# Attention followed by a four-expert layer: all four experts' second layer as seven block products, with side work moved between VectorE and GpSimd

## Chip, cores and metric

The kernel runs on one core of a Trainium2 chip. The metric is the device time of one execution in microseconds (us); smaller is better. Every figure below comes from the page of one profiled execution of the kernel before, from its trace, or from the runs' times.

## What is computed

The reference, cut to what matters. First, attention with pooled keys and values (8 batches, 8 heads, 576 queries, width 64, keys and values averaged in groups of 8, so 72 of them):

```python
k_p = k.reshape(B, H, Sp, pool, D).mean(axis=3)
v_p = v.reshape(B, H, Sp, pool, D).mean(axis=3)
scores = scale * np.matmul(q, k_p.transpose(0, 1, 3, 2))
attn = softmax(scores)
x = (attn @ v_p) rearranged to (4608, 512)
```

Then four experts, each a two-layer network of width 512, 1024, 512, weighted by probabilities:

```python
p = domain_probs / (domain_probs.sum(-1, keepdims=True) + 1e-09)
for e in range(4):
    h = np.maximum(x @ w1[e], 0.0)
    out += p[:, e:e + 1] * (h @ w2[e])
```

## The kernel before

**Chunks and steps.** The 4608 tokens are nine chunks `c` of 512: chunk `b` for `b` below 8 holds the first 512 queries of batch `b`; chunk 8 holds the 64 left over from each of the eight batches. A step `s` is a pair `(c, e)`, with `s = 4c + e`. In step `s` TensorE computes the first layer ("up") of `(c, e)` and, interleaved with it, the second layer ("down") of the step before it. While chunk `c` goes through its four steps, the attention of batch `c + 1` is worked in between.

**Block products.** A product of two matrices cut into 2 by 2 blocks can be formed from seven block products in place of eight (the method of Strassen and Winograd), if sums and differences of blocks, here called forms, are ready. The up layer is done so from step 2 on, except for step 4: `product` (L652) issues 4 matmuls of 256 columns for one block and one of two halves `j`, so 2 x 7 x 4 = 56 for a step. It needs forms of the weights (`combine_w1`, L600 to L603) and of x (`forms_of`, L616: four differences of 128x512). The down layer comes in two ways. The plain way (`down`, L850) issues 32 matmuls of 512 columns, and `merge` adds each of the four results into `acc` (VectorE, L867; on ScalarE for expert 0, L864). The split way (`up_down`, with `half`, L777) issues 56 matmuls of 256 columns, again in two halves `j`. It needs forms of w2 (`combine_w2`, L640 to L643, in the tile `w2_t`, with one block of w2 overwritten) and of the hidden layer (`sums_of`, L717 to L720: s1, the difference that overwrites a21, s2 and S4, each 128x1024). The function `splits` says which steps' down layer is split: experts 0, 1 and 2 from chunk 2 on, and experts 1 and 2 of chunk 1, which makes 23 steps.

**The end of a split step.** The last first-layer result of a step comes through `relu_sum` (L700), and the sums follow at once on VectorE: s1, a21, s2, S4. In the next step TensorE runs product 1, half 1, products 5 and 6, and then half 7, which reads a21 as overwritten; half 6 follows with s2, half 5 with s1, and last of the j = 0 half, half 3 with S4.

**Order.** Every engine's order is written out by hand. `up_down` and `between` pass 16 numbered points a step; `attention(c)` lists pieces of work with `add(n, ...)`, and a piece stands at point 2n + 1 of its chunk, so that eight values of n make a step and 32 a chunk. Every second point is also a slot, which takes one piece off the queue `forms_due`. The pieces of the attention of batch `b` are:
- `load_half` (L96): keys and values arrive by DMA issued on GpSimd, in two halves, the second of which is added to the first by the DMA. It can only go when the first has landed.
- `fold_parts` (L211, L216, L219): the rest of the pooling, on VectorE, for keys (into `kp`) and for values (into `vps`).
- `keys` (L233), `queries` (L251), `turn` (L412), `rem_turn`: transposes by DMA from SP, which also issues the stores of the output (L875, L879).
- `loads_wait` (L240): a one-element copy on GpSimd that waits for the transposed keys, and so holds back the loads queued behind it.
- `scores` (L268 on TensorE, L272 on ScalarE), `context` (L391), `divide` (L372, L373), and, in every odd chunk, the same for the left-over queries (`rem_...`).

**Preparation.** The weights arrive in the first 60 us or so. Their forms are made in steps 1 to 8; those of w2 for expert 2 are made on GpSimd in step 5, all others on VectorE.

Of the kernel before, what the change touches and what calls it, by code (L numbers as in the profile page):

```python
# [18 lines left out]
def kernel(  # L19
# [16 lines left out]
    POOL = 8  # L36
# [12 lines left out]
    SPLIT = (0, 1, 2)  # L49
# [25 lines left out]
    w2_t = wpool.tile([P, len(SPLIT), 3, FCH // 2, TH], BF16, name="w2_t")  # L75
# [9 lines left out]
    def load_kv(b, src, nm):  # L85
        wide = (w2_t[0:SP].rearrange("p a b f d -> p (a b f d)")[:, 0:H * POOL * D] if nm == "vraw"
# [70 lines left out]

    NBLK = NCH * NR
# [48 lines left out]
    def fold_parts(nm, b, hs, last):  # L207

        def first():
            raw = raws[(nm, b)]  # L210
            nc.vector.tensor_add(out=raw[:, hs, 0:4, :], in0=raw[:, hs, 0:4, :],  # L211
                                 in1=raw[:, hs, 4:8, :])

        def rest():
            raw = raws[(nm, b)]
            nc.vector.tensor_add(out=raw[:, hs, 0:2, :], in0=raw[:, hs, 0:2, :],  # L216
                                 in1=raw[:, hs, 2:4, :])
            for out in last(hs):
                nc.vector.tensor_add(out=out, in0=raw[:, hs, 0, :], in1=raw[:, hs, 1, :])  # L219
# [3 lines left out]
    def key_parts(b):  # L223
        return [part for hs in halves for part in fold_parts(
            "kraw", b, hs, lambda hs: [kp[0:SP, hs, dup, :] for dup in range(2)])]

    def value_parts(b):
        return [part for hs in halves for part in fold_parts(
            "vraw", b, hs, lambda hs: [vps[b % 3][:, hs, 0:D]])]
# [209 lines left out]
    def rem_scores(i):  # L439
        qTr = state.pop(("qTr", i))  # L440
        two = two_banks()
        for bb in range(2):
# [9 lines left out]
        expTr = apool.tile([SP, 2, 2, NPAIR, REM], BF16, name="expTr", bufs=1)  # L452
        nc.scalar.activation(
            out=expTr[:].rearrange("j a b h t -> j (a b h t)"),
# [77 lines left out]
    def attention(c):  # L532
# [8 lines left out]
        if c % 2:  # L541
            i = c // 2
            add(18, lambda: rem_queries(i))
            add(23, lambda: rem_scores(i))
            add(26, lambda: rem_context(i))
            add(27, lambda: rem_turn(i))
        if b == B:
            for part in forms_of(B):
                add(31, part)
            return plan  # L550
        more, far = b + 1 < B, b + 2 < B
        if c == 1:
# [4 lines left out]
            for half in range(2):  # L557
                add(2 + half, lambda half=half: load_half(b + 1, k, "kraw", half))
# [5 lines left out]
        else:  # L564
            for pair in range(NPAIR):
                add(5 + pair, lambda pair=pair: scores(b, pair))
            add(0, key_parts(b)[1], lambda: keys(b))
            for n, part in enumerate(value_parts(b)):
                add(3 + n, part)
            if more:  # L570
                add(0, lambda: loads_wait(b))
                for half in range(2):
                    add(2 + 2 * half, lambda half=half: load_half(b + 1, k, "kraw", half))
# [4 lines left out]
        if more:  # L578
# [446 lines left out]
```

## Time and profile before

| | |
|---|---|
| median of 3 runs | 514.88 us (514.63 to 516.45) |
| profiled execution | 514.31 us; its span from first to last instruction is 512.6 us |
| granted TensorE clock | 0.999 of full speed |
| TensorE matmul busy | 498.9 us, 97% of the span |
| VectorE busy | 370.5 us, 72% |
| ScalarE busy | 274.1 us, 53% |
| GpSimd busy | 72.4 us, 14% |
| DMA | 41.62 MB, mean 81 GB/s |

"Busy" is the time in which an engine executes an instruction. The profile names instructions by engine (PE is TensorE, PEld its loading of weights, DVE VectorE, ACT ScalarE, POOL GpSimd, SP SyncE), by line of the kernel and by tiles, output before input. The chain of waits follows the work that ended last back from the end: at each step to what released an instruction, or to the instruction ahead of it on its engine. The timeline lists instructions in order of time, with start and duration, and in brackets how long the engine had been idle before and who released it.

### The profile page before, as it was taken

The numbers are of one execution on the slowest core, as the hardware profiler recorded it, in microseconds if no ns is written. First come the engines' busy times: TensorE is split into PE (matmuls) and PEld (weight loads), VectorE is DVE, ScalarE is ACT, GpSimd is POOL, SyncE is SP. The second block draws the span as 40 slices with busy tenths as digits, with TensorE's granted clock in tenths as the row PEclk, the third lists the DMA queues.
The fourth block names the chain that finished last, engine by engine and source line by source line (L and its number), as shares of the span: only waits on it lengthen the run. The fifth ranks groups of instructions, "written<-read, shape, count | busy, mean of one in ns | idle before, by whom it ended". The sixth has DMA issues, their size and how long they took to land.

```text
span 512.6 us, 10563 instructions
## 1 busy us (share of the span) xinstructions
PE 498.9 (97%) x4339; PEld 379.0 (74%) x4339; DVE 370.5 (72%) x693; ACT 274.1 (53%) x495; POOL 72.4 (14%) x85
## 2 busy tenths in 40 slices
PE   8899989999999999999999999999999999999996
PEld 4746544578768876888688868886888788868883
DVE  2335788878888877877787868787778567766774
ACT  3654434655466547654566556564765456535650
POOL 8362102740112001100220021000000000000000
PEclk9999999999999999999999999999999999999999
DMA  9999999775179217940597049501210110011003
GB/s 135 205 206 205 202 147 181 125 80 64 41 110 143 27 26 110 137 58 10 107 128 86 1 100 126 58 12 55 62 22 1 42 54 1 12 42 42 0 2 84
DMA packets 82977, 41.62 MB, mean 81 GB/s; under 512 B 46560, under 2 KB 78304, under 8 KB 82928
## 3 DMA queue, kind: packets, MB, share of 16 engines
q0 software_dynamic: 41584, 22.65, 34.8%
q1 hardware_dynamic: 41344, 18.29, 17.6%
q8 instruction: 34, 0.56, 0.4%
q14 instruction: 15, 0.12, 0.1%
HBM read 45.16 MB, written 9.44 MB: 107 GB/s over the span
## 4 chain that ended last, share of the span: by engine, by line
PE 77%; DMA 9%; DVE 8%; POOL 2%; issue 1%; ACT 1%; DVEq 0%; POOLq 0%; ACTq 0%
PE g_ps L652 34%; PE u_ps L777 26%; PE o_ps L850 12%; DMA w_bf<-in_moe_w_dram 4%; DMA q_sb<-in_q_dram 4%; DVE acc L783 2%; PE two L268 2%; DVE H_sb L700 2%; PE h_ps L670 1%; PE two L391 1%; POOL w_bf L148 1%; DVE x_tok L373 1%; DVE h_s L717 1%; DMA xT<-x_tok 1%; DVE xf L616 1%
## 5 line engine op out<-in xcount | busy, mean ns | idle before, releaser
L652 PEld LDWEIGHTS <-w_bf 128*128 128x128 bf16 x1848 | 176.8, 98 | 39.4 <-issue 6.5
L652 PE MATMUL g_ps<-xf,w_bf 128*128 128x256 bf16 x1056 | 148.4, 272 | 1.7 <-ACT g_ps L789 0.7
L696 ACT COPY r<-g_ps 128x512 f32<-128x512 f32 x152 | 89.1, 586 | 77.1 <-PE g_ps L652 66.5
L700 DVE CUSTOM_DVE_ANT_0 H_sb<-g_ps,r 128x512 bf16<-128x512 f32 x152 | 104.3, 687 | 32.4 <-ACT r L696 29.6
L783 DVE SCALAR_TENSOR_TENSOR acc<-u_ps,p_all,acc 128x256 f32<-128x256 f32 (+1 forms) x156 | 91.3, 587 | 41.9 <-ACT u_ps L805 40.9
L850 PE MATMUL o_ps<-w_bf,H_sb 128*128 128x512 bf16 x416 | 104.0, 379 | 0.0
L652 PE MATMUL g_ps<-xT,w_bf 128*128 128x256 bf16 x696 | 101.8, 273 | 0.0
L703 ACT ACTIVATE H_sb<-g_ps 128x512 bf16<-128x512 f32 x112 | 66.8, 597 | 25.0 <-PE g_ps L652 25.0
L777 PEld LDWEIGHTS <-H_sb 128*128 128x128 bf16 x736 | 70.0, 98 | 11.7 <-DVE H_sb L718 2.7
L777 PE MATMUL u_ps<-w_bf,H_sb 128*128 128x256 bf16 x552 | 75.5, 273 | 0.2
L850 PEld LDWEIGHTS <-H_sb 128*128 128x128 bf16 x416 | 40.5, 98 | 31.5 <-issue 0.2
L777 PEld LDWEIGHTS <-h_s 128*128 128x128 bf16 x552 | 54.0, 98 | 6.3
L777 PE MATMUL u_ps<-w_t,h_s 128*128 128x256 bf16 x368 | 55.2, 273 | 0.0
L789 ACT COPY g_ps<-g_ps 128x512 f32<-128x512 f32 x46 | 26.3, 571 | 48.2 <-PE g_ps L652 48.1
L867 DVE SCALAR_TENSOR_TENSOR acc<-o_ps,p_all,acc 128x512 f32<-128x512 f32 x44 | 32.8, 745 | 8.9 <-PE o_ps L850 8.8
L272 ACT ACTIVATE expT<-two 72x1024 bf16<-72x1024 f32 x28 | 28.6, 1021 | 12.5 <-PE two L268 12.5
L805 ACT COPY u_ps<-u_ps 128x256 f32<-128x256 f32 x46 | 16.4, 357 | 25.5 <-PE u_ps L777 25.2
L777 PE MATMUL u_ps<-w_t,H_sb 128*128 128x256 bf16 x184 | 27.7, 273 | 0.0
L777 PE MATMUL u_ps<-w_bf,h_s 128*128 128x256 bf16 x184 | 27.6, 273 | 0.0
L373 DVE TENSOR_TENSOR x_tok<-two,inv 128x512 bf16<-128x512 f32 x32 | 22.1, 691 | 1.1
L807 DVE TENSOR_SCALAR acc<-u_ps,p_all 128x512 f32<-128x512 f32 x14 | 10.5, 750 | 14.1 <-ACT u_ps L805 14.1
L717 DVE TENSOR_TENSOR h_s<-H_sb 128x1024 bf16<-128x1024 bf16 x23 | 15.7, 684 | 5.3 <-ACT H_sb L703 5.3
(112 smaller groups left out, 386.4 us busy)
## 6 DMA issues: line engine op xcount, KB each, us to landing
out_dram<-acc SPq DMA_DIRECT2D x32, 256.0 KB, 2.3
w_bf<-in_moe_w_dram POOLq DMA_DIRECT2D x16, 256.0 KB, 9.8
w_bf<-in_moe_w_dram POOLq DMA_DIRECT2D x4, 1024.0 KB, 16.8
q_sb<-in_q_dram POOLq DMA_DIRECT2D x7, 512.0 KB, 9.3
raw_kv<-in_k_dram POOLq DMA_DIRECT2D x10, 288.0 KB, 6.7
raw_kv<-in_v_dram POOLq DMA_DIRECT2D x10, 288.0 KB, 9.0
raw_kv<-in_k_dram POOLq DMA_DIRECT2D x2, 576.0 KB, 15.8
w_t<-in_v_dram POOLq DMA_DIRECT2D x2, 576.0 KB, 14.3
```

The lines of the kernel that those rows point to most:

```text
L272: nc.scalar.activation(out=state[("expT", b)][:, 2 * pair:2 * pair + 2].rearrange("j h r s p -> j s (h r) p"), in_=two[0:SP].rearrange("j ...
L373: nc.vector.tensor_tensor(out=x_tok[:], in0=c_ps[:, :, :, 0:D], in1=inv[:].unsqueeze(3).to_broadcast([P, 2, NPAIR, D]), op=ALU.mult,)
L652: nc.tensor.matmul(bank[:, t, :], lhsT=w1_bf[:, e, block, kc, lo:lo + P], rhs=x[:, kc, :], start=(first and t == 0 and kc == 0), stop=(t = ...
L696: nc.scalar.copy(out=r[:], in_=ps[:])
L700: nc.vector._custom_dve(TENSOR_ADD_SAT, out=out, in0=ps[:], in1=r[:], s0=BIG, s1=0.0)
L703: nc.scalar.activation(out=out, in_=ps[:], func=ACT.Relu)
L717: lambda: add(out=s1, in0=a21, in1=a22),
L777: nc.tensor.matmul(out, lhsT=lhs[0][:, lhs[1] + f, lhs[2]], rhs=rhs[0][:, rhs[1] + f, rhs[2]], start=(start and f == 0), stop=(f == FCH // ...
L783: nc.vector.scalar_tensor_tensor(out=acc, in0=ps, scalar=prob, in1=acc, op0=ALU.mult, op1=ALU.add,)
L789: nc.scalar.copy(out=s[:], in_=g[:])
L850: nc.tensor.matmul(sums[r][:], lhsT=hidden[(c, e)][:, fc, r * P:(r + 1) * P], rhs=w2_bf[:, e, fc, :], start=(fc == 0), stop=(fc == FCH - 1),)
L867: nc.vector.scalar_tensor_tensor(out=dst, in0=o_ps[:], scalar=prob, in1=dst, op0=ALU.mult, op1=ALU.add,)
```

## The change

**Which steps are split.** `splits` becomes true from (1, 2) up to (8, 2): all four experts of chunks 2 to 7, experts 2 and 3 of chunk 1, experts 0 to 2 of chunk 8. That is 29 steps. Expert 1 of chunk 1 becomes plain; expert 3 of chunks 1 to 7 becomes split. `w2_t` grows to four experts, and the values that borrow it on arrival lie in the part of experts 2 and 3. The last step, expert 3 of chunk 8, stays plain and needs w2 as it was, so the overwritten block is loaded again in step 33. The stores of the output, which `merge` issued, are issued from `up_down` when the expert is the last.

**What changes engine.** S4 goes to GpSimd. From chunk 2 on the forms of x are made on GpSimd, and the last of them is written over a block of x that is no longer needed, in place of a fourth tile. The folds of keys are on GpSimd from batch 3 on. The forms of w2 are all on VectorE, over steps 1 to 8.

**What moves.** In `attention`, `loads_wait` stays for batch 2 only. Scores move to n = 2, 4, 6, 8, loads of keys to 4 and 8, key folds of the next batch to 16 (they were at 31 and at 0 of the next chunk), loads of values to 21 and 27, `keys` to 24, loads of queries to 28, the forms of x to 25 (they were at 22, 25, 28 and 29). The left-over queries of the last chunk move from n = 18, 23, 26, 27 to 2, 10, 13, 14, and their exponentials share a buffer with the others.

The diff, cut to its core:

```diff
-    w2_t = wpool.tile([P, len(SPLIT), 3, FCH // 2, TH], BF16, name="w2_t")
+    w2_t = wpool.tile([P, E, 3, FCH // 2, TH], BF16, name="w2_t")
...
+    def reload_w2(e):
+        rows = moe_w2[e].rearrange("(fc p) d -> p fc d", p=P)
+        nc.gpsimd.dma_start(out=w2_bf[:, e, 4:8, TH:DM], in_=rows[:, 4:8, TH:DM])
...
     def key_parts(b):
+        engine = nc.vector if b == 2 else nc.gpsimd
         return [part for hs in halves for part in fold_parts(
-            "kraw", b, hs, lambda hs: [kp[0:SP, hs, dup, :] for dup in range(2)])]
+            "kraw", b, hs, lambda hs: [kp[0:SP, hs, dup, :] for dup in range(2)], engine)]
...
         if c % 2:
             i = c // 2
-            add(18, lambda: rem_queries(i))
-            add(23, lambda: rem_scores(i))
-            add(26, lambda: rem_context(i))
-            add(27, lambda: rem_turn(i))
+            q_at = 15 if b < B else 2
+            for n, piece in zip((0, 8, 11, 12), (rem_queries, rem_scores, rem_context, rem_turn)):
+                add(q_at + n, lambda piece=piece: piece(i))
+        parts = forms_of(b, nc.gpsimd)
+        add(25, *parts)
...
             for pair in range(NPAIR):
-                add(5 + pair, lambda pair=pair: scores(b, pair))
-            add(0, key_parts(b)[1], lambda: keys(b))
+                add(2 + 2 * pair, lambda pair=pair: scores(b, pair))
             for n, part in enumerate(value_parts(b)):
-                add(3 + n, part)
-            if more:
-                add(0, lambda: loads_wait(b))
-                for half in range(2):
-                    add(2 + 2 * half, lambda half=half: load_half(b + 1, k, "kraw", half))
+                add(4 + n, part)
...
         if more:
+            add(4, lambda: load_half(b + 1, k, "kraw", 0))
             add(11, lambda: queries(b + 1))
-            add(31, key_parts(b + 1)[0])
-            for half in range(2):
-                add(17 + 2 * half, lambda half=half: load_half(b + 1, v, "vraw", half))
+            add(8, lambda: load_half(b + 1, k, "kraw", 1))
+            add(16, *key_parts(b + 1))
+            add(21, lambda: load_half(b + 1, v, "vraw", 0))
+            add(27, lambda: load_half(b + 1, v, "vraw", 1))
+            add(24, lambda: keys(b + 1))
         if far:
-            add(19, lambda: (load_q(b + 2), load_q_rem(b + 2)))
-        for n, part in enumerate(forms_of(b)):
-            add((22, 25, 28, 29)[n], part)
+            add(28, lambda: (load_q(b + 2), load_q_rem(b + 2)))
...
         def last():
-            new(at(1, 0), t[1])
+            engine.tensor_sub(out=at(0, 1), in0=at(1, 1), in1=at(0, 1))
...
     def splits(c, e):
-        return e in SPLIT and (c > 1 or c == 1 and e > 0)
+        return (1, 2) <= (c, e) < (B, E - 1)
...
-            lambda: sub(out=s4, in0=a12, in1=s2),
+            lambda: nc.gpsimd.tensor_sub(out=s4, in0=a12, in1=s2),
...
             elif s == 4:
-                w, x = combine_w1(0), combine_x(1)
-                forms_due.extend(w[:2] + combine_w1(1) + x[:1] + [lambda: (x[1](), w[2]())])
+                v2, x = combine_w2(1), forms_of(1)
+                forms_due.extend(v2[:2] + combine_w1(1))
+                forms_due.extend([lambda: (x[0](), x[1]()), lambda: x[2]()])
             elif s == 5:
-                forms_due.extend(w[3:] + nothing[:2] + combine_w2(1))
-                placed.setdefault(at + 5, []).extend(combine_w2(2, nc.gpsimd))
+                x[3]()
+                forms_due.extend(u[3:] + nothing[:2] + combine_w2(2))
+            elif s == 6:
+                v3 = combine_w2(3)
+                forms_due.extend(nothing[:1] + v3[:1] + nothing[:2] + v3[1:])
+            elif s == 7:
+                forms_due.extend(nothing[:1] + v2[2:3] + nothing[:3] + v2[3:])
             elif s == 8:
-                forms_due.extend(nothing[:1] + combine_w2(0))
+                forms_due.extend(nothing[:1] + w[3:])
+            elif s == E * B + 1:
+                reload_w2(E - 1)
```

Steps 1 and 2 make the forms of chunk 0's x and the first forms of expert 0's weights in the same manner.

## The prediction

> **What bounds the kernel now.** I read the busy table first, then the chain of waits, then busy time by stage, then timelines of the stages that differ. The busy table and the chain's shares by engine, from the page:
>
> ```profile
> PE 498.9 (97%) x4339; PEld 379.0 (74%) x4339; DVE 370.5 (72%) x693; ACT 274.1 (53%) x495; POOL 72.4 (14%) x85
> ...
> PE 77%; DMA 9%; DVE 8%; POOL 2%; issue 1%; ACT 1%; DVEq 0%; POOLq 0%; ACTq 0%
> ```
>
> TensorE is the bound, but "busy" counts overlapping matmuls, so I check it with issue rates. The chain in order of time (start, us, what) has pure runs of each kind:
>
> ```profile
> 154.71 0.87 PE g_ps L652 x8
> 155.58 0.26 PE two L391 x8
> 155.84 1.31 PE u_ps L777 x12
> ...
> 194.60 0.34 PE two L268 x4
> ...
> 501.09 6.92 PE o_ps L850 x32
> ```
>
> So a 256-column matmul takes 0.109 us (1.31/12) and a 512-column one 0.216 us (6.92/32). Chunk 2 lasts from 148.83 to 201.78 us in that chain, 52.95 us, and issues 224 of L652, 168 of L777 (together 392 x 0.109 = 42.8), 32 of L850 (6.9), 16 of L268 (1.4) and 32 of L391 (1.05): 52.2 us. Only 0.8 us of a chunk is anything but issue. Fewer TensorE columns therefore pay in full, as long as nothing else grows into the path.
>
> The nearest thing to the path is VectorE at a step's end:
>
> ```profile
> 172.64 0.60 DVE H_sb L700
> 173.23 0.61 DVE h_s L717
> 173.84 0.02 issue
> 173.87 0.70 DVE H_sb L718
> 174.57 0.05 issue
> 174.62 1.48 PE u_ps L777 x12
> ```
>
> relu_sum, s1 and a21 run without a gap and release half 7. From product 3's end TensorE has half 3, product 1, half 1, products 5 and 6 to do, 5 x 0.44 = 2.2 us; VectorE needs 0.6 + 0.6 + 0.7 plus hand-overs, about 2.1. There is no slack: whatever holds s1 or a21 stalls TensorE by as much.
>
> One stage is not TensorE-bound, 94 to 107 us (step 5), where GpSimd makes expert 2's forms. Its timeline:
>
> ```profile
> 94.19 2.68 POOL L640 TENSOR_TENSOR w_t<-w_bf 128x1024 bf16<-128x1024 bf16 x1
> 95.16 2.26 DVE L640 TENSOR_TENSOR w_t<-w_bf 128x1024 bf16<-128x1024 bf16 x1
> 96.95 2.46 POOL L641 TENSOR_TENSOR w_t<-w_bf,w_t 128x1024 bf16<-128x1024 bf16 x1
> 98.18 0.68 DVE L700 CUSTOM_DVE_ANT_0 H_sb<-g_ps,r 128x512 bf16<-128x512 f32 x1
> 98.78 1.18 DVE L641 TENSOR_TENSOR w_t<-w_bf,w_t 128x1024 bf16<-128x1024 bf16 x1
> ```
>
> VectorE's difference, 0.68 us elsewhere (L600), takes 2.26 and 1.18, ending each time 0.55 us after GpSimd's instruction ends. L700, which reads one input from PSUM, keeps its 0.68. From 93.73 to 107.11 us TensorE issues work worth 11.6 us at the rates above, and takes 13.4: 1.8 us lost.
>
> **What the Trainium skill says.** "SBUF — State Buffer", section "SBUF: two separate sides": VectorE and GpSimd share a port pair as an exclusive lock; a VectorE instruction with two SBUF inputs and a GpSimd instruction that reads SBUF exclude each other for a whole instruction. The four lines above agree. "GPSIMD Engine Reference", section 3.1: about 2.6 cycles an element at 1.2 GHz for two inputs, so an estimate of 2.2 us for 1024 elements; the trace has 2.46 to 2.68 (mean 2.57), which leaves 0.35 fixed. "TensorE: Matmul & The Clock Gate", "Back-to-back issue gap": 216 ns for 512 columns, as here.
>
> **The change, part by part.**
>
> 1. *Split downs.* 29 instead of 23: net six steps swap 32 x 0.216 = 6.92 us of L850 for 56 x 0.109 = 6.11 of L777. All of it is on the path: 6 x 0.81 = **-4.9 us**. In front of it stands only the tie at the step's end, which those steps have already (or had, in plain form, when the next down was split).
>
> 2. *Step 5.* No GpSimd differences there any more, and (1, 1) is not split, so no sums at its end either. VectorE gets back 1.58 + 3 x 0.49 = 3.05 us of blocking and 2.7 of sums in a 13-us stage that it bound. Of TensorE's 1.8 us I count **-1.5**; the rest stays with the contexts' waits for x_tok. Bounds: 0 and -1.8.
>
> 3. *VectorE.* A split down costs it per step 2 x (0.746 + 2 x 0.477 + 0.746) = 4.9 us of L783 against 4 x 0.745 = 3.0 of L867, but 4 rather than 6 relu_sums (-1.4), and 3 sums of 0.69 after it. It loses S4 (0.69 a step), forms of x (4 x 0.415 a chunk) and key folds (2 x 0.41 + 4 x 0.284 = 2.0 a chunk). A chunk's busy time goes down. In the fullest changed step (e = 0) it has 4 x 0.687 + 4.9 + 2.1 + 1.4 (values) = 11.1 us for about 13.5. ScalarE has 2 x 3.6 + 4 x 1.02 = 11.3 there. Both fit: **0**. The forms of x no longer stand in front of the closing sums; I count nothing for that (bound -0.2 a chunk).
>
> 4. *GpSimd's compute.* Sizes not shown are estimated as 0.35 plus the slope: 1.46 us for 512 elements, 0.9 for 256. A chunk then has S4 4 x 2.57, forms 4 x 1.46 and key folds 2 x (1.46 + 2 x 0.9) = 6.6, with gaps 23 us, plus 8 us of issuing DMAs. What matters is where it lies. Counting from product 1 of step e = 2: s2 is done at 2.4 (in the trace product 1 at 212.99, L719's end at 215.37). S4 2.4 to 5.1; key folds to 12.1. The step lasts 12.6, and the next s1 comes 0.36 later (L717 at 213.36): 12.95. **Margin 0.85 us.** Values' first load is issued to 13.5; S4 of e = 2, ready at 15.0, to 17.6; forms to 23.7, next s1 at 25.3: margin 1.6. Then values' second load to 25.1, loads of queries to 26.8, S4 of e = 3 from 27.4 to 30.0, wanted by half 3 at 31.0: margin 1.0. VectorE's only other two-input SBUF work is the value folds at about 33. So at my sizes GpSimd's work is covered: **0**. Without the cover it costs what part of a GpSimd instruction is left, once or twice a step end.
>
> 5. *Waits and queues.* S4 waits on VectorE with K and V loads behind it, forms wait on the transposed x (n = 20, landing 4.1 us). Removing loads_wait frees GpSimd's queue (122.4 us of waiting). The key transpose (landing 2.7 us) now shares the DMAs with the first V load, but has from n = 24 to 34, 16 us. V's second half leaves at about 23.7 and lands 6.7 to 9 later (medians of the K and V issues), at 30.4 to 32.7, against the fold at 33: tight, VectorE would wait 0 to 1 us, with 1.5 us to spare before the next accumulation. SP's stores move from L867 to L783, with the flips four n later. **0**, bound +1 a chunk for five chunks.
>
> 6. *Steps 6 to 8.* Three w2 forms (v3[0], v2[2], w[3]) fall beside key folds or S4 on GpSimd, each blocked by 0 to 2.6 us in the early part of a step, where VectorE otherwise waits for ScalarE (L783: 40.9 us over 28 waits, 1.5 each). I take **+0.7** of 0 to +4. Reloading w2 (512 KB, less than two steps before use) is hidden; its issue is under 1 us on an idle GpSimd.
>
> Sum against the profiled execution: 514.31 - 4.9 - 1.5 + 0.7 = 508.6. The median of the runs is 0.6 above that execution: **509.2 us**.
>
> **The rivals.**
>
> *Slower: GpSimd's instructions reach the step's end.* For it: the tie has no slack, margins are 0.85 and 1.6 us, and no row shows a 72-partition or 512-element difference on GpSimd. Against: 2.57 us repeated within 4%, and the estimate scales only the slope. It decides when key folds take over 12% more than 7.0 us. At half as much again (10.5 us and 9.1 for the forms), s1 and a21 each meet on average half an instruction: 2 x 0.6 us in five chunks with key folds, 2 x 0.75 in seven with forms, 16.5 us in all: **525.7 us**.
>
> *No change: the gain is given back on the other engines.* The converted step is filled by VectorE and ScalarE (11.1 and 11.3 of 13.5 us), four exponentials of 1.02 us stand in ScalarE's queue between copies that TensorE waits for, and S4 or values come late. If each of six such steps loses as much as it won, 0.8 us: 509.2 + 4.9 = **514.1 us**. Against: scores at n = 2, 4, 6, 8 lie after the copies, not ahead of them.
>
> *The split isn't worth its columns.* 56 loads of weights of 98 ns instead of 32 could show; but the runs of L777 above have the same loads and go at 0.109. Not likely, and it ends at no change too.
>
> **How the numbers follow.** My forecast 0.71 (506 to 512), no change 0.16 (512 to 516), slower 0.13 (516 to 527). A measurement of this kernel can tell about 0.5%, 2.6 us, from no change. Faster by over that (below 512.3): 0.73; slower (above 517.4): 0.12; between: 0.15. The range 506 to 515 takes the forecast whole, with the bounds of parts 2, 3 and 6, and most of the second case, and leaves the slower one out.
>
> **What would show it.** After: L777 with 29 x 56 = 1624 matmuls and L850 with 224; GpSimd near 210 us; VectorE near 350; a chunk near 52.1 us; no L640 beside a GpSimd difference in step 5. Right in part 4 if L717 and L718 keep 0.69 us; wrong if their means rise to 1 us or more, or if GpSimd's 72x512 takes over 1.65. Wrong in part 5 if VectorE waits for raw_kv, or TensorE's half 3 for S4.

## The result, and the profile after

| | before | changed |
|---|---|---|
| median of the runs | 515.1 us (514.63 to 516.45, 4 runs) | 507.82 us (506.38 to 508.62, 4 runs) |
| ratio, with its 95% interval | | 0.985 (0.982 to 0.988) |
| profiled execution | 514.31 us, span 512.6 us | 508.62 us, span 506.9 us |
| the same kernel, five more runs beside the experiments | | 506.85 us (506.34 to 508.0), ratio 0.984 (0.982 to 0.985) |

The change makes the kernel about 1.5% faster. The forecast was 509.2 us with a range of 506 to 515.

The changed kernel's page has the busy table and the chain's shares by engine that were shown of before:

```profile
PE 494.3 (98%) x4483; PEld 392.6 (77%) x4483; DVE 355.5 (70%) x650; ACT 287.6 (57%) x531; POOL 179.7 (35%) x165
...
PE 90%; DVE 5%; DMA 1%; ACT 1%; issue 1%; POOL 1%; POOLq 0%; ACTq 0%
```

TensorE executes more matmuls (4483 for 4339) in less time, since the split way needs fewer columns in total (56 times 256 where the plain one has 32 times 512). VectorE has lost 15 us, and GpSimd has gained 107. On the chain TensorE rises from 77% to 90% and VectorE falls from 8% to 5%. By tiles, L769 (the former L777) has 1624 matmuls (696 + 464 + 232 + 232) and L855 (the former L850) 224, as the change intends.

Step 5 is no longer VectorE's. This is the chain in order of time (start, us, what) at the place where the kernel before showed VectorE's L640 to L643 between its relu_sums; the piece that follows begins each time where the last one ends:

```profile
96.44 0.54 PE g_ps L647 x4
96.98 0.86 PE o_ps L855 x4
97.84 0.26 PE two L395 x8
98.10 0.88 PE g_ps L647 x8
```

The end of a split step, VectorE's timeline:

```profile
224.31 0.69 DVE L695 CUSTOM_DVE_ANT_0 H_sb<-g_ps,r 128x512 bf16<-128x512 f32 x1
224.91 0.68 DVE L712 TENSOR_TENSOR h_s<-H_sb 128x1024 bf16<-128x1024 bf16 x1
225.63 0.69 DVE L713 TENSOR_TENSOR H_sb<-H_sb 128x1024 bf16<-128x1024 bf16 x1
226.24 0.68 DVE L714 TENSOR_TENSOR h_s<-h_s,H_sb 128x1024 bf16<-128x1024 bf16 x1
```

relu_sum, s1, a21 and s2 keep their 0.68 us. Over all 29 split steps the longest s1 is 0.686 us and the longest a21 0.694: GpSimd never held one up. What GpSimd did in the step before this end is in its own timeline (start, us, instruction, and in brackets how long it had been idle and for whom):

```profile
214.49 2.12 POOL L715 TENSOR_TENSOR h_s<-H_sb,h_s 128x1024 bf16<-128x1024 bf16 x1 [9.95 <-DVE h_s L714]
216.58 1.14 POOL L219 TENSOR_TENSOR raw_kv<-raw_kv 72x512 bf16<-72x512 bf16 x1
217.80 1.29 POOL L222 TENSOR_TENSOR kp<-raw_kv 72x256 bf16<-72x256 bf16 x2
...
221.51 0.87 POOL L95 DMA_DIRECT2D raw_kv<-in_v_dram  x1
227.08 2.11 POOL L715 TENSOR_TENSOR h_s<-H_sb,h_s 128x1024 bf16<-128x1024 bf16 x1 [4.70 <-DVE h_s L714]
```

The other half of the key folds, left out here, takes as long as the half shown. S4 and all key folds are done at 221.57, 3.3 us before s1 at 224.91. The bracket of the first line matters for all that follows: GpSimd had stood idle for 9.95 us, waiting for VectorE's s2. S4 is not only work of 2.12 us. It is also the place where GpSimd's queue stops until a step's critical end is over.

**Step by step.** The clearest account comes from the start of each step, taken as its first copy of g_ps on ScalarE. In both kernels steps 9 and 35 begin with such a copy. Before, they begin at 147.21 and 489.29 us; in the changed kernel's second profiled execution (506.73 us), at 145.32 and 481.74. So 1.9 us are won up to step 9, and 342.08 - 336.42 = 5.66 us between. From the last step to the end nothing changes (the span is 512.6 against 505.0, 7.6 us in all). A chunk without left-over queries takes 52.05 us (13.66 + 13.46 + 12.6 + 12.33); it took 52.95.

The 5.66 us are not evenly spread. Each of the five stretches of four steps from step 9 to step 29 is shorter by 0.89 to 0.92 us. The stretch from step 29 to step 33 is shorter by 1.18 us (51.64 before, 50.46 after), and the last two steps are the same within 0.04 us.

### The profile page after: what moved, and what is told of

It is laid out like the page before. It is cut to its first block, busy times and chain, and to the rows that moved or that the text cites. A ratio compares the mean times of both kernels' runs of the same rounds, so it can differ in the third digit from the quotient of the medians.

```text
span 506.9 us, 10946 instructions
## 1 busy us (share of the span) xinstructions
PE 494.3 (98%) x4483; PEld 392.6 (77%) x4483; DVE 355.5 (70%) x650; ACT 287.6 (57%) x531; POOL 179.7 (35%) x165
## 4 chain that ended last, share of the span: by engine, by line
PE 90%; DVE 5%; DMA 1%; ACT 1%; issue 1%; POOL 1%; POOLq 0%; ACTq 0%
PE g_ps L647 38%; PE u_ps L769 35%; PE o_ps L855 8%; PE h_ps L665 3%; PE two L272 2%; PE h_ps L678 2%; PE two L395 1%; DMA q_sb<-in_q_dram 1%; DVE H_sb L695 1%; DVE x_tok L377 1%; DVE acc L872 1%; DVE acc L753 0%; ACT xT L432 0%; PE two L452 0%; POOL H_sb L107 0%
## 5 line engine op out<-in xcount | busy, mean ns | idle before, releaser
L753 DVE SCALAR_TENSOR_TENSOR acc<-u_ps,p_all,acc 128x512 f32<-128x512 f32 (+1 forms) x204 | 121.3, 594 | 77.0 <-ACT u_ps L806 72.7
L715 POOL TENSOR_TENSOR h_s<-H_sb,h_s 128x1024 bf16<-128x1024 bf16 x29 | 61.4, 2119 | 231.1 <-DVE h_s L714 231.1
L647 PE MATMUL g_ps<-xT,w_bf 128*128 128x256 bf16 x928 | 130.0, 273 | 0.0
L647 PE MATMUL g_ps<-xf,w_bf 128*128 128x256 bf16 x792 | 109.8, 272 | 0.6 <-ACT g_ps L790 0.4
L695 DVE CUSTOM_DVE_ANT_0 H_sb<-g_ps,r 128x512 bf16<-128x512 f32 x140 | 96.4, 689 | 12.8 <-ACT r L691 8.2
L769 PEld LDWEIGHTS <-H_sb 128*128 128x128 bf16 x928 | 86.8, 98 | 18.2 <-DVE H_sb L713 4.7
L769 PE MATMUL u_ps<-w_bf,H_sb 128*128 128x256 bf16 x696 | 95.3, 273 | 0.4 <-DVE H_sb L713 0.3
L769 PEld LDWEIGHTS <-h_s 128*128 128x128 bf16 x696 | 68.1, 98 | 7.9
L769 PE MATMUL u_ps<-w_t,h_s 128*128 128x256 bf16 x464 | 69.6, 273 | 0.0
L855 PE MATMUL o_ps<-w_bf,H_sb 128*128 128x512 bf16 x224 | 54.7, 379 | 0.0
L806 ACT COPY u_ps<-u_ps 128x256 f32<-128x256 f32 x58 | 20.7, 357 | 32.8 <-PE u_ps L769 32.6
L855 PEld LDWEIGHTS <-H_sb 128*128 128x128 bf16 x224 | 21.7, 98 | 18.9
L769 PE MATMUL u_ps<-w_t,H_sb 128*128 128x256 bf16 x232 | 35.0, 273 | 0.0
L769 PE MATMUL u_ps<-w_bf,h_s 128*128 128x256 bf16 x232 | 34.8, 273 | 0.0
L794 ACT COPY u_ps<-u_ps 128x256 f32<-128x256 f32 x58 | 21.1, 363 | 0.0
```

Source lines behind the costliest of these rows:

```text
L647: nc.tensor.matmul(bank[:, t, :], lhsT=w1_bf[:, e, block, kc, lo:lo + P], rhs=x[:, kc, :], start=(first and t == 0 and kc == 0), stop=(t = ...
L695: nc.vector._custom_dve(TENSOR_ADD_SAT, out=out, in0=ps[:], in1=r[:], s0=BIG, s1=0.0)
L715: lambda: nc.gpsimd.tensor_sub(out=s4, in0=a12, in1=s2),
L753: nc.vector.scalar_tensor_tensor(out=acc, in0=ps, scalar=prob, in1=acc, op0=ALU.mult, op1=ALU.add,)
L769: nc.tensor.matmul(out, lhsT=lhs[0][:, lhs[1] + f, lhs[2]], rhs=rhs[0][:, rhs[1] + f, rhs[2]], start=(start and f == 0), stop=(f == FCH // ...
L794: nc.scalar.copy(out=two[:, lo], in_=one[:, lo])
```

## The experiments

Each kernel is the changed one with the edit shown, unless it says that it is the one before. Ratios are to runs of the kernel before on the same chip, whose median was between 514.7 and 515.7 us. Steps are named by their expert e.

**1. What are the six split steps worth?** They are taken out again, and all else stays.

```diff
-        return (1, 2) <= (c, e) < (B, E - 1)
+        return (1, 2) <= (c, e) < (B, E - 1) and (e < E - 1 or c == 1)
...
-            elif s == E * B + 1:
+            elif s == 9:
                 reload_w2(E - 1)
```

> The changed kernel, but expert 3 of chunks 2 to 7 has its second layer done plainly again (23 split steps, as before; the overwritten block of w2 is loaded again in step 9 in place of step 33). Everything else, the moves to GpSimd too, stays. Theory A, the gain is TensorE's columns: each of six steps gets 0.81 us longer, a chunk goes from 52.04 to 52.85 us, and the whole is 4.9 us slower than the changed kernel, about 2.5 us faster than the kernel before. Theory B, the gain is VectorE's relief at the steps' ends: little is lost, 0 to 2 us, since the work stays on GpSimd.

Measured: 512.37 us (512.04 to 512.7), ratio 0.995 (0.993 to 0.996). Against the changed kernel (506.85) that is 5.5 us; against experiment 2's kernel (507.47), which ran with it on the same chip, 4.9, but two of that kernel's four runs lie near 508 us (see the end). The starts of the steps are the better measure. From step 7 to step 35 this kernel takes 369.3 us and the changed one 363.7, so the difference, 5.6, lies in the chunks, where it should. The forecast had 4.9 for these columns. The rest is no saving of columns: four of the six chunks are longer by 1.06 us, where the columns give 0.81 (the other two by 0.7). In one of the plain steps, step 16, the chain shows the last exponential ahead of a first-layer result at the step's end:

```profile
250.21 1.02 ACT expT L276
251.23 0.49 ACT H_sb L698
```

The changed places of the scores suit a split step better than a plain one. The other parts of the change alone leave 512.37, which is 2.8 us below the kernel before on that chip (515.21). In the profiled executions it is 1.8 us (spans of 510.8 and 512.6), and 1.7 of that lies ahead of step 9. From step 9 to step 35 this kernel takes 342.00 us and the kernel before 342.08: without the six split steps, what was moved is worth next to nothing in the chunks, in sum.

**2. Does the place of the key folds on GpSimd matter?** They are put at n = 21, five values of n later.

```diff
-            add(16, *key_parts(b + 1))
+            add(21, *key_parts(b + 1))
```

> The changed kernel, but the key folds on GpSimd stand at n = 21 in place of 16, so that their 5 us lie across the end of step e = 2 in five chunks. If the lock and the missing slack are as I read them: s1 or a21 (0.68 us each) take up to 1.1 us more there, half 7 comes as much later, 0.5 to 1 us a chunk, 2.5 to 5 us in all, and more where S4 is pushed behind. If GpSimd's work is harmless wherever it lies: no difference (under 0.5 us), s1 and a21 unchanged.

Measured: 507.47 us (506.63 to 508.05), no change. The test is inconclusive: the folds ran when they had run before. GpSimd's timeline in this kernel:

```profile
213.96 2.12 POOL L715 TENSOR_TENSOR h_s<-H_sb,h_s 128x1024 bf16<-128x1024 bf16 x1 [9.95 <-DVE h_s L714]
216.06 1.15 POOL L219 TENSOR_TENSOR raw_kv<-raw_kv 72x512 bf16<-72x512 bf16 x1
```

The folds follow S4 at once. GpSimd works off its own list in order, and here a later place in the written order moved nothing, since no entry between waits for something. The attempt to move a piece by its place alone failed a second time in the next run.

**3. The kernel before, with GpSimd's forms of expert 2 placed 16 points, one whole step, later.**

```diff
-                placed.setdefault(at + 5, []).extend(combine_w2(2, nc.gpsimd))
+                placed.setdefault(at + 21, []).extend(combine_w2(2, nc.gpsimd))
```

> The kernel before, but expert 2's forms of w2 are made on GpSimd one step later (step 6 in place of step 5). If the blocking in step 5 is what TensorE loses there: VectorE's differences L640 to L643 of step 5 fall from 2.26 and 1.18 to 0.69 us, and 1 to 1.5 us of TensorE's 1.8 come back; step 6 must not lose it again. If VectorE is simply overfull in step 5: no change, 0 to 0.3 us.

Measured: 515.44 us (514.16 to 517.68, 12 runs), ratio 1.000 (0.999 to 1.002). Inconclusive for the same reason: GpSimd made the forms from 96.2 to 106.5 us all the same, once its DMA issues were through, and stood against three of the same four instructions of VectorE (1.04 to 1.18 us each; only the first one kept its 0.68).

**4. The kernel before, without GpSimd's forms of expert 2.** This is the test that experiment 3 should have been. The four differences are left out, and GpSimd fills the tile with zeros instead, ahead of everything.

```diff
+        nc.gpsimd.memset(w2_t[:, 2].rearrange("p a f d -> p (a f d)"), 0.0)
...
-                placed.setdefault(at + 5, []).extend(combine_w2(2, nc.gpsimd))
```

> The kernel before, without expert 2's forms of w2: GpSimd fills their tile with zeros at the start, so that expert 2's output is not the reference's. b1_gps_later did not move GpSimd's work (its queue ran ahead and did it at 96 to 106 us all the same). Here step 5 has no GpSimd difference at all. If the blocking is what costs TensorE time there: VectorE's four differences take 0.69 us each, the stretch from 93.7 to 107.1 us gets 1 to 1.7 us shorter, and the whole kernel as much. If VectorE is overfull in step 5 anyhow (four forms of w2, four contexts, the sums): under 0.5 us.

Measured: 513.0 us (511.94 to 514.03, 12 runs), ratio 0.995 (0.994 to 0.997): 2.2 us faster. Step 5's end comes at 105.75 instead of 107.11 us, 1.36 earlier, and VectorE's forms, which took 2.26 and 1.18 us in the kernel before, have their normal time in this one's timeline:

```profile
95.23 0.68 DVE L640 TENSOR_TENSOR w_t<-w_bf 128x1024 bf16<-128x1024 bf16 x1
98.53 0.68 DVE L641 TENSOR_TENSOR w_t<-w_bf,w_t 128x1024 bf16<-128x1024 bf16 x1
```

So 1.36 of the 1.8 us that TensorE lost in step 5 were GpSimd's blocking of VectorE.

**5. Are GpSimd's margins real, and is the blocking?** Three differences of 72x1024 that nobody needs are put behind the key folds, into a free part of the keys' buffer.

```diff
+    def filler(b):
+        free = raws[("kraw", b)][:, 4:8].rearrange("j h r d -> j h (r d)")
+        nc.gpsimd.tensor_sub(out=free, in0=w2_bf[0:SP, 0, 0:4, 0:TH], in1=w2_bf[0:SP, 1, 0:4, 0:TH])
...
             add(16, *key_parts(b + 1))
+            for _ in range(3):
+                add(16, lambda: filler(b + 1))
```

> The changed kernel with three more differences (72 partitions, 1024 elements, about 2.1 us each) on GpSimd right behind the key folds, into a buffer that is free then, in five chunks. In e4_keys_late the key folds ran as early as ever, since nothing in GpSimd's queue held them back, so that run did not test the step's end; here GpSimd is busy to about 16 us into step e = 2, across s1 and a21 at 12.9 to 14.3. If the lock holds and the end of a step has no slack: s1 or a21 take 1 to 2 us more than 0.68 in those five steps, half 7 is late by 1.5 to 2.7 us, and the kernel is 7 to 13 us slower than the changed one. If GpSimd's work is harmless where it lies: under 1 us.

Measured: 520.91 us (518.18 to 522.74), ratio 1.011 (1.006 to 1.015), 14 us more than the changed kernel. In the profiled execution 12.4 us of it are paid at the end of the step e = 2 in the five chunks with key folds: the steps that follow are longer by 1.3, 4.4, 2.0, 2.7 and 2.0 us. GpSimd's timeline, then VectorE's at the same end of a step, which the changed kernel passes with 0.68 and 0.69:

```profile
225.75 6.85 POOL L237 TENSOR_TENSOR raw_kv<-w_bf 72x1024 bf16<-72x1024 bf16 x3
```

```profile
228.41 0.69 DVE L701 CUSTOM_DVE_ANT_0 H_sb<-g_ps,r 128x512 bf16<-128x512 f32 x1
229.02 1.60 DVE L718 TENSOR_TENSOR h_s<-H_sb 128x1024 bf16<-128x1024 bf16 x1
230.66 2.49 DVE L719 TENSOR_TENSOR H_sb<-H_sb 128x1024 bf16<-128x1024 bf16 x1
```

Each of the two sums waits for the end of one of GpSimd's instructions, and TensorE waits with them. relu_sum (L701), which takes an input from PSUM, ran against them too and isn't lengthened. This is what the Trainium skill, "SBUF — State Buffer", section "SBUF: two separate sides", says of the lock that the two engines share, and here the trace agrees with it: 0.69 us becomes 2.49. The mechanism of the slower rival is real. It only didn't occur.

**6. All three moved pieces of work back on VectorE, at the changed places.**

```diff
-        engine = nc.vector if b == 2 else nc.gpsimd
+        engine = nc.vector
...
-        parts = forms_of(b, nc.gpsimd)
+        parts = forms_of(b, nc.vector)
...
-            lambda: nc.gpsimd.tensor_sub(out=s4, in0=a12, in1=s2),
+            lambda: sub(out=s4, in0=a12, in1=s2),
```

> The changed kernel, but S4, the forms of x and the key folds are all back on VectorE, at the places of the changed kernel. Theory A: TensorE's columns stay saved; VectorE has 0.7 us more in each split step and 1.7 to 2.0 in steps e = 2 and e = 3, which fill to about 12 of 12.3 us, so up to 0.2 us a chunk comes back at steps' ends: 1 to 2 us slower than the changed kernel. Theory B: the moves are what the gain is made of, so at least 5 us slower, near the kernel before.

Measured: 519.28 us (518.72 to 520.39), ratio 1.009 (1.007 to 1.010). It is 12.4 us slower than the changed kernel, and slower than the one before. I had thought 1 to 2 us: VectorE has room for this work by its total. The timeline of VectorE shows what a total doesn't:

```profile
217.82 0.69 DVE L715 TENSOR_TENSOR h_s<-H_sb,h_s 128x1024 bf16<-128x1024 bf16 x1
218.43 0.41 DVE L219 TENSOR_TENSOR raw_kv<-raw_kv 72x512 bf16<-72x512 bf16 x1
218.88 0.49 DVE L222 TENSOR_TENSOR kp<-raw_kv 72x256 bf16<-72x256 bf16 x2
...
220.15 0.74 DVE L753 SCALAR_TENSOR_TENSOR acc<-u_ps,p_all,acc 128x512 f32<-128x512 f32 x1
```

The key folds come in one piece between 218.43 and 220.2 us, and the accumulation at L753 stands behind them. It reads a PSUM bank that TensorE needs next, and the chain passes from L753 (to 220.90) to TensorE's L769 at 220.94. The steps e = 2 with key folds grow by 0.85 us each (four of them from step 10 on, 3.4 in all), and the steps e = 3, where the forms of x stand in the same place, by 1.0 to 1.4 (six, 6.9 in all). With 1.6 in step 7 that makes the 11.9 us that these steps differ by. Another 1.7 us lie ahead of step 7, and experiment 10 shows what they are.

**7. S4 alone back on VectorE.** It has 0.69 us there, in a step of 12 to 14.

```diff
-            lambda: nc.gpsimd.tensor_sub(out=s4, in0=a12, in1=s2),
+            lambda: sub(out=s4, in0=a12, in1=s2),
```

> The changed kernel with S4 alone back on VectorE. S4 stands behind a21 and s2, so half 7 does not wait for it, but the accumulation acc_u behind it comes 0.69 us later, and with it the PSUM bank that it frees. Theory A: 0 to 1 us slower. Theory B: 29 x 0.1 to 0.3 us, 3 us or more slower.

Measured: 517.16 us (515.1 to 519.38, 15 runs), ratio 1.003 (1.001 to 1.004), 10 us slower than the changed kernel. Not S4's 0.69 us does that. The steps of chunk 8, where GpSimd has nothing else to do, keep their 12.33 us. Eight of the steps from 11 to 27 are longer, by 0.6 to 1.8 us each and 9.4 in all. One of them shows GpSimd at the wrong time; its timeline, and VectorE's beside it:

```profile
224.57 1.15 POOL L616 TENSOR_TENSOR xf<-xT 128x512 bf16<-128x512 bf16 x1 [23.05 <-DMA xT<-x_tok]
225.81 2.71 POOL L616 TENSOR_TENSOR xf<-xT,xf 128x512 bf16<-128x512 bf16 x2
```

```profile
227.54 1.52 DVE L713 TENSOR_TENSOR H_sb<-H_sb 128x1024 bf16<-128x1024 bf16 x1
228.99 1.64 DVE L714 TENSOR_TENSOR h_s<-h_s,H_sb 128x1024 bf16<-128x1024 bf16 x1
```

Without S4 nothing in GpSimd's queue waits for the step's end. The bracket now names the transfer of x: as soon as x lands, GpSimd begins the forms, 2.2 us ahead of s1 (226.78), and runs right across a21 and s2, which take 1.52 and 1.64 us for 0.69.

**8. S4 on VectorE, but GpSimd waits for it.** If that reading is right, a wait must do as well as the work. GpSimd copies one element of S4 to a place that nobody reads.

```diff
-            lambda: nc.gpsimd.tensor_sub(out=s4, in0=a12, in1=s2),
+            lambda: (sub(out=s4, in0=a12, in1=s2),
+                     nc.gpsimd.tensor_copy(out=mark[:], in_=s4[0:1, 0, 0:1])),
```

> The changed kernel with S4 on VectorE, as in e2_s4_vector, and in S4's place on GpSimd a copy of one element of S4, which only makes GpSimd's queue wait there for the end of the step. In e2_s4_vector the steps of chunk 8, where GpSimd has nothing else to do, kept their 12.33 us, while steps with key folds or forms nearby grew by 0.6 to 1.8 us. If it was lost because nothing held GpSimd's queue back any more, so that key folds and forms ran into the end of the step before: this kernel is within 1.5 us of the changed kernel, a1 and a21's differences keep 0.69 us. If S4's 0.7 us on VectorE is what costs: it stays near 517 us.

Measured: 506.64 us (506.28 to 506.95), ratio 0.983 (0.981 to 0.985): all 10 us come back. GpSimd's timeline:

```profile
225.54 0.18 POOL L716 COPY mark<-h_s 1x1 bf16<-1x1 bf16 x1 [6.63 <-DVE h_s L715]
225.75 1.15 POOL L616 TENSOR_TENSOR xf<-xT 128x512 bf16<-128x512 bf16 x1
```

The forms start after S4, the longest a21 is 0.693 us again, and every step from 7 to 34 takes what it takes in the changed kernel, within 0.01 us. Which engine computes S4 is worth nothing that can be measured here. That GpSimd is held until the sums are through is worth 10 us.

**9. The split alone, with the side work on VectorE and spread as in the kernel before.** Scores, loads and folds stand at their old points; the left-over queries of the last chunk alone stay early.

```diff
-        engine = nc.vector if b == 2 else nc.gpsimd
+        engine = nc.vector
...
-                add(2 + 2 * pair, lambda pair=pair: scores(b, pair))
+                add(5 + pair, lambda pair=pair: scores(b, pair))
+            add(0, key_parts(b)[1], lambda: keys(b))
...
-            add(16, *key_parts(b + 1))
+            add(31, key_parts(b + 1)[0])
...
-        parts = forms_of(b, nc.gpsimd)
-        add(25, *parts)
+            for n, part in enumerate(forms_of(b)):
+                add((22, 25, 28, 29)[n], part)
...
-            lambda: nc.gpsimd.tensor_sub(out=s4, in0=a12, in1=s2),
+            lambda: sub(out=s4, in0=a12, in1=s2),
```

> The changed kernel's splits (29) and its w2 forms, with everything else of the attention as in the kernel before: S4, forms of x and key folds on VectorE, spread over the same points as before, scores and loads where they were. e3_all_vector piled 1.7 and 4 us of VectorE's work up in one place; this one does not. Theory A, columns: 1 to 3 us slower than the changed kernel, about 509 to 511 us, VectorE's fuller e = 0 step costing that. Theory B, VectorE's relief is what makes room for the split: at 514 us or more, no gain over the kernel before.

Measured: 522.12 us (522.03 to 523.59), ratio 1.014 (1.011 to 1.018), 7 us slower than the kernel before. Nearly all of it lies in the first step of the five chunks with key folds: 16.3 us instead of 13.66 (17.1 instead of 14.1 in chunk 2), 13.6 us of the 15.3 by which steps 7 to 34 are longer than in the changed kernel. The chain in such a step:

```profile
247.68 0.35 DVE raw_kv L219
...
248.06 0.49 DVE kp L222 x2
248.55 0.67 DVE acc L759
...
249.26 0.60 PE u_ps L775 x4
...
255.64 1.03 ACT expT L276
...
259.84 0.59 ACT g_ps L796
...
260.47 0.60 PE g_ps L653 x4
```

Two things stand on it; the kernel before, with a plain down in this step, has 0.8 us of anything but issue in a whole chunk. The key folds stand ahead of the accumulation that frees a bank (to 249.22), and the exponentials, one at each n from 5 to 8, stand ahead of ScalarE's copy of g_ps, for which TensorE waits. How the 2.6 us divide between the two wasn't tried apart.

**10. All on VectorE, but spread.** As in experiment 6, with the key folds as two pieces and the forms as two pairs.

```diff
-        parts = forms_of(b, nc.gpsimd)
-        add(25, *parts)
+        parts = forms_of(b)
+        add(24, *parts[:2])
+        add(28, *parts[2:])
...
-            add(16, *key_parts(b + 1))
+            for n, part in zip((16, 20), key_parts(b + 1)):
+                add(n, part)
```

> The changed kernel with S4, forms of x and key folds all on VectorE, as in e3_all_vector, but not piled up: each half of the key folds (1 us) and each pair of forms (0.8 us) stands alone at n = 16, 20, 24 and 28, right after half 1 and products 5 and 6 of a half step, where VectorE otherwise waits 1.5 to 2.5 us for ScalarE's copy. If what counts is where VectorE's work stands, not on which engine: the steps keep the changed kernel's 13.7, 13.4, 12.6 and 12.3 us, with 1 to 1.5 us lost in step 6, where four w2 forms, sums and key folds meet: 507 to 509 us. If VectorE simply has no room for it all: steps e = 2 and e = 3 grow by 0.8 to 1.4 us as in e3_all_vector, 515 us or more.

Measured: 510.76 us (509.52 to 511.36), ratio 0.991 (0.987 to 0.994). Without any help from GpSimd in the chunks the split is faster than the kernel before. It is about 2 us more than I had expected if only the place counted. From experiment 6 to here, by place alone, it is 8.5 us; from here to the changed kernel, by engine, 3.9. What is left is in part the same effect, in four steps with a pair of forms at n = 24, 12.93 us for 12.33. VectorE's timeline there:

```profile
176.64 0.42 DVE L618 TENSOR_TENSOR xf<-xT 128x512 bf16<-128x512 bf16 x1
177.09 0.43 DVE L618 TENSOR_TENSOR xf<-xT,xf 128x512 bf16<-128x512 bf16 x1
177.43 0.74 DVE L755 SCALAR_TENSOR_TENSOR acc<-u_ps,p_all,acc 128x512 f32<-128x512 f32 x1
```

Four times 0.6 is 2.4 us, and step 7 adds 0.5. Another 1.75 us lie ahead of step 7, and nearly all of that (1.6) arises in step 6. There the first key folds meet VectorE before their keys have landed, and VectorE stands idle for 4 us in front of a relu_sum; its timeline:

```profile
108.87 0.42 DVE L219 TENSOR_TENSOR raw_kv<-raw_kv 72x512 bf16<-72x512 bf16 x1 [4.00 <-DMA raw_kv<-in_k_dram]
```

In experiment 6 the same instruction waits 3.29 us. In the changed kernel it is GpSimd that waits for this transfer (7.05 us in the second profiled execution), and TensorE doesn't notice. So part of what the engine is worth here is only who waits.

**11. The changed kernel again, and 12. with four more warming matmuls early on.** In some profiles TensorE runs for a few microseconds at half clock soon after the start (more on this at the end). Experiment 12 asks whether a denser beginning prevents it.

```diff
         context_first(1, 1)
+        warm(2)
         turn_here(0, 0)
         context_first(2, 0)
         context_first(2, 1)
+        warm(2)
```

> The changed kernel itself, beside e9_warm on the same chip: median 507.8 us, its runs in two groups near 506.5 and 508.2, if the dip of the clock is what parts them.

> The changed kernel with four more idle matmuls (512 columns, results unused) in gaps of TensorE at 16 to 19 us, where the profiled execution then shows 3.4 us at half clock. If that dip comes because TensorE has too little work there: the dip is absent, and the runs that are now near 508.2 come at 506.5, the median 1 us lower. If the dip does not depend on these gaps: runs stay in two groups, the median within 0.5 us of the changed kernel, and 0.5 us or so is added by the matmuls.

Measured: 506.85 us (506.34 to 508.0) and 506.75 us (506.47 to 507.01), five runs each: no difference in the median. The runs with the additional matmuls lie within 0.54 us, but with five of them that doesn't show that the cause is removed. No version clearly beats the changed kernel: this one and experiment 8's are within 0.3 us of it.

## Why the prediction was right

The direction and the mechanism of the two main parts were right; the size was a quarter too small. The sum of 508.6 us for the profiled execution meets the 508.62 of the first one partly by chance: that execution contains a stretch at half clock that costs some 1.5 us, and the second one had 506.73. Held against that, the forecast's gain of 5.7 us was too small by 1.9: it left out 0.7 us ahead of step 5 and 0.8 in the chunks, and put the loss after step 5 at 0.7 where 0.3 came out. By its parts:

- **Part 1, the columns, -4.9.** Right. Every stretch of four steps that holds a newly split step is shorter by at least 0.89 us, where the columns give 0.81, and experiment 1, which takes the six split steps out, loses 5.6. The runs of L769 on the chain still go at 1.31 us for 12: the additional loads of weights cost nothing, so that rival falls. The 216 ns for 512 columns is what this trace shows in a run of 32; the section that the prediction names beside it gives that figure as the gap of an isolated matmul, and about 131 ns for a sustained stream, which nothing here shows.
- **Part 2, step 5, -1.5.** Right in mechanism and size: what lasted from 93.73 to 107.11 us takes from 93.02 to 104.92 in the second profiled execution, 1.5 us less, and experiment 4, which removes nothing but GpSimd's forms, wins 1.36 us there. Its median gains 2.2, more than the stage, and the profiles don't say where the rest comes from. VectorE's 2.7 us of sums, which the forecast counted beside the blocking, are still there in experiment 4, so their going bought about 0.1 at most.
- **Part 3, VectorE, 0 with a bound of -0.2 a chunk.** Right within its bound in the middle chunks: they win 0.08 to 0.11 us each beyond the columns, and what wins it wasn't traced. In the stretch from step 29 to step 33 it was too small: 0.37 us beyond the columns. There the forms of the left-over x stood on the chain of the kernel before, and TensorE's L652 waited for the last of them. Its chain:

```profile
451.62 0.34 DVE xf L616
...
451.99 0.44 DVE xf L616
...
452.47 0.61 PE g_ps L652 x4
```

GpSimd makes them now. Steps 31 and 32 win 0.73 us beyond the columns, but some matmuls of the left-over queries have moved from step 31 to step 29, and steps 29 and 30 are 0.36 us longer. The forecast counted nothing for it, though these lines were in the profile before. How much is due to the engine of the forms and how much to the places of the left-over queries wasn't tried apart.

- **Part 4, GpSimd's work is hidden, 0.** Right in what it says, wrong in its sizes, on the safe side. The changed kernel's groups (count, then busy time and mean ns):

```profile
L715 POOL TENSOR_TENSOR h_s<-H_sb,h_s 128x1024 bf16<-128x1024 bf16 x29 | 61.4, 2119 | 231.1 <-DVE h_s L714 231.1
...
L222 POOL TENSOR_TENSOR kp<-raw_kv 72x256 bf16<-72x256 bf16 x20 | 13.2, 681 | 0.8
L219 POOL TENSOR_TENSOR raw_kv<-raw_kv 72x512 bf16<-72x512 bf16 x10 | 11.5, 1146 | 12.6 <-DMA raw_kv<-in_k_dram 12.6
```

  The forecast had 2.57, 0.9 and 1.46 us; they are 2.12, 0.68 and 1.15. The 2.57 was read where VectorE stood against each of those instructions: a number with contention in it was taken for the cost of the operation. The slope is (2119 - 1146) / 512 = 1.90 ns an element, 2.3 cycles at 1.2 GHz, below the 2.6 cycles that the Trainium skill, "GPSIMD Engine Reference", section 3.1, gives. So the key folds take 5.0 us and not 7.0, the margin ahead of s1 is 3.3 us in the step shown (0.8 us longer than the one that the forecast reckoned with) and not 0.85, and GpSimd is busy for 179.7 us and not 210. In experiment 7's step the same margin is gone.
- **Part 5, waits and queues, 0.** Right. The second half of the values lands 6.6 us after its issue (the forecast had 6.7 to 9), and VectorE never waits for it; TensorE never waits for S4. But this part saw S4's wait only as a burden on what is queued behind it, "with K and V loads behind it". Experiments 7 and 8 show that the same wait is what keeps GpSimd off the step's end, and that it is worth 10 us. Part 4's margins were reckoned with that wait in place, so the number came out right, but the working never says that they hang on it.
- **Part 6, steps 6 to 8, +0.7.** A loss of this size is there, but not by the forecast's mechanism. GpSimd's instructions did block two forms of w2 in step 6 of the first profiled execution (to 0.84 and 1.14 us from 0.68), and none in the second, and the steps that follow are equal in both. But steps 7 and 8 take 27.27 us together. They took 27.22 before, with one plain down more, so 0.81 us should have gone; and steps 15 and 16, which do the same but for the forms of w2, take 26.39. Between the two steps VectorE is on the chain of the changed kernel, and in steps 15 and 16 it isn't there at all (second profiled execution):

```profile
129.82 0.60 DVE w_bf L638
130.42 0.40 DVE acc L753
130.82 0.59 DVE H_sb L695
131.41 0.61 DVE h_s L712
```

  The form of w2 (L638) has its normal 0.68 us. By this chain it costs TensorE time by standing ahead of the closing relu_sum and s1, not by being blocked; no run tries it alone. The rest of step 6 wins 0.6 us against it, so that 0.3 are lost up to step 9.

Together, by stretches, with the second profiled execution: 0.7 us are won ahead of step 5, for which no part of the forecast stands and which no run explains; 1.5 in step 5; from there to step 9 0.3 are lost; between steps 9 and 35 the columns are 4.9 and the rest is 0.8 (0.47 in the five stretches up to step 29, 0.37 in the next, less 0.04). That makes the 7.6 us, and 514.31 - 7.6 = 506.7.

**The rivals.** *Slower, by GpSimd at the step's end*: experiment 5 shows the mechanism, and the rival's way of pricing it. By half an instruction for each of s1 and a21, experiment 5's instructions (6.85 / 3 = 2.28 us) give an estimate of 2.28 us a chunk and 11.4 in five; the steps show 12.4. The rival's 16.5 can't be held against it, since it also counted the forms of x. Experiment 7 shows a second way into it that the forecast didn't name. *No change, the gain given back on VectorE and ScalarE*: this was nearer than its chance of 0.16 says. Experiment 9 is that case, with 2.6 us in a step and not the 0.8 that the rival allowed. The rival did name the exponentials between ScalarE's copies, but its 0.8 was what a split step wins and not what such a queue costs, and it didn't name the key folds ahead of the accumulation. The changed kernel escapes it by place: in experiment 10, with folds and forms on VectorE but the scores two values of n apart and the folds at n = 16 and 20, the same step keeps its 13.66 us.

**What stays open.** Which of key folds and exponentials carries more of experiment 9's loss; what wins 0.7 us ahead of step 5; and what starts the stretch at half clock.

## What to carry to other kernels

When an engine is at its limit, work removed from it pays in full only if the work beside it stays out of the few instructions that release it: ask of each moved piece what it stands ahead of in its queue, not whether the engine has room. A queue without waits runs ahead of the order in which it was written; if its work may not meet a certain moment, it needs an instruction there that waits, and a one-element copy of 0.18 us is enough. Take an operation's price from a row where nothing contends with it.

## What was not expected of the hardware

In some executions TensorE runs at half clock for about 3.4 us near 20 us after the start, and in others of the same kernel it doesn't. The first profile's row of granted clocks has an 8 in that slice, which is 12.7 us long; in finer windows the granted clock is 0.50 in each half microsecond from 19 to 22 us, where the second profile has 1.00. In the timelines of TensorE, the same 16 matmuls are these, first in the changed kernel's first profiled execution, then in its second:

```profile
19.13 3.48 PE L678 MATMUL h_ps<-xT,w_bf 128*128 128x256 bf16 x16 [0.41 <-ACT xT L432]
```

```profile
18.42 1.91 PE L678 MATMUL h_ps<-xT,w_bf 128*128 128x256 bf16 x16 [0.41 <-ACT xT L432]
```

They take 1.6 us longer, and this execution is 1.9 us longer as a whole, nearly all of it already there at step 7. The changed kernel's nine runs fall into a group near 506.7 us (506.3 to 507.4) and one near 508.3 (508.0 to 508.6). That the stretch is what parts them was seen in the two profiled ones alone. The profiles of experiments 2, 4 and 7 have such a stretch too; that of the kernel before and those of the other experiments don't. A difference of 1.5 us between two profiled executions is therefore no evidence for an edit until their early timelines are laid side by side.
